# Output projection of the second attention block: both column halves per token tile, with one weight load asked for each pair of matmuls

## The chip, the cores and the metric

The kernel runs on one core of a Trainium2 chip. The metric is device time in microseconds (us), and lower is better. A "ratio" is the mean time of one kernel's fast runs over the mean time of the other kernel's fast runs in the same rounds, with a 95% interval, so it isn't quite the ratio of the medians that are quoted beside it.

The engines are named as in the profile: PE is the matmul engine (TensorE), PEld its weight loads, ACT is ScalarE, DVE is VectorE, POOL is GpSimd and SP is the engine that issues most DMAs (166 of the 176 issues in the trace before).

## The reference

Two independent attention blocks, A and B, have the same shapes. Their outputs are put side by side.

```python
# B=16 sequences, 32 query tokens, D=1024, 32 query heads, 4 key/value heads, 512 cached keys, head size 128; bf16
q = (x @ wq) split into heads
scores = q @ k_cache.T * 128 ** -0.5        # each key/value head serves 8 query heads
o = softmax(scores) @ v_cache
out = concat_heads(o) @ wo                  # [512 tokens, 4096] @ [4096, 1024]
result = concatenate([out_A, out_B], axis=-1)
```

The change touches the last product of block B alone. It is computed for four tiles of 128 tokens. Each tile needs 32 products (one per head) for each of two column halves of 512.

## The kernel before

PE interleaves two streams. In each "slot" it computes the scores of one (sequence, key/value head) and the weighted values of an earlier one. Between them it takes some 6.6 products from a generator, `stream()`, which delivers the query projections and then the output projections. So there is always a dense product ready while ACT and DVE work on the softmax.

```python
def f_units(pr, tt, n0, width, eng):                 # one token tile, one column half
    ps = psum.tile([P, NW], FP32, name="f_ps", tag="proj")      # "proj": 2 PSUM banks
    nh, off = divmod(n0, NW)
    for h in range(HQ):                              # 32 heads
        nc.tensor.matmul(
            ps[:, 0:width],
            lhsT=oT[pr, tt][:, h, :],                # stationary operand: attention output of a head
            rhs=wo_tiles[pr, nh, h // REP][:, h % REP, off:off + width],
            start=(h == 0), stop=(h == HQ - 1),
        )
        if h == HQ - 1:
            o_sb = outp.tile([P, NW], BF16, name="o_sb")
            nc.scalar.copy(out=o_sb[:, 0:width], in_=ps[:, 0:width])
            eng.dma_start(out=..., in_=o_sb[:, 0:width])
        yield

def run(units, n):
    for _ in range(n):
        next(units, None)
# ... (cut: query projections, scores, values, softmax sums)
for i in range(total_slots + LAG):
    if live:
        do_loads(i)        # DMA issues planned for this slot
        scores(i)          # 4 matmuls of 256 columns, then the exponential on ACT
    run(units, 1)
    # ...
    values(i - LAG)        # 4 matmuls of 256 columns
    # ...
    run(units, 5)
    # ...
```

Each stationary operand `oT[1, tt][:, h, :]` is thus loaded twice, once for either column half, at times that lie far apart. (For the last token tile it is three times: its second half is computed as two quarters of 256 columns.)

## Time and profile before

| | before |
|---|---|
| time, median of the first 3 runs | 343.30 us (342.92 to 343.53) |
| span of the profiled run | 341.2 us |
| PE busy | 335.2 us, 98% |
| weight loads (PEld) | 213.6 us, 63%, 2121 of them |
| ACT and DVE busy | 54% and 78% |

The first fence holds lines of the page of the kernel before: busy time with share and number of instructions of each engine, the granted TensorE clock in 40 equal slices (9 stands for 90% or more), the chain of work that ended last, and four groups of instructions. A group's line gives the line of the program, engine, operation, operands, count, then busy us and mean ns of one, then the idle time of the engine just before.

```profile
PE 335.2 (98%) x2082; PEld 213.6 (63%) x2121; DVE 265.5 (78%) x336; ACT 185.9 (54%) x209; POOL 46.7 (14%) x206
...
PEclk9999999999999999999999999999999999999999
...
PE 98%; issue 1%; ACT 0%; ACTq 0%
...
L320 PE MATMUL f_ps<-wo_sb,oT 128*128 128x512 bf16 (+1 forms) x525 | 128.2, 366 | 0.6
...
L425 PE MATMUL ob<-p_sb,v_sb 128*128 128x256 bf16 x512 | 76.8, 273 | 0.8
...
L320 PEld LDWEIGHTS <-oT 128*128 128x128 bf16 x544 | 53.2, 98 | 35.3
...
L425 PEld LDWEIGHTS <-v_sb 128*128 128x128 bf16 x512 | 50.1, 98 | 20.0
```

PE is never idle for long, its clock is full in every slice (the trace's record of it begins at 5.1 us), and the chain that ended last is PE nearly from end to end. A matmul's recorded time (366 ns on average here, 379 for one of 512 columns) is longer than the distance to the next start, so the records of successive matmuls overlap. The pace is read from starts. This is the timeline of PE alone (start, duration, then the group and its count), from the same trace:

```profile
200.32 1.46 PE L320 MATMUL f_ps<-wo_sb,oT 128*128 128x512 bf16 x6
201.61 0.60 PE L357 MATMUL s_ps<-qT,kT 128*128 128x256 bf16 x4
202.05 0.38 PE L320 MATMUL f_ps<-wo_sb,oT 128*128 128x512 bf16 x1
202.26 0.60 PE L425 MATMUL ob<-p_sb,v_sb 128*128 128x256 bf16 x4
```

Six products of 512 columns start at 200.32 and the next group at 201.61: 1.29 us / 6 = 215 ns each. Four of 256 columns take 201.61 to 202.05, 110 ns each. Taken from all records, the distance is 215 or 216 ns after 512 columns (mean 215.8) and 109 or 110 ns after 256 (mean 109.2). The 256 columns between them thus cost 106.7 ns, which is 2.4 columns per ns, and some 2.5 ns of either distance is left that doesn't grow with the columns. This rate and this remainder are what the recorded texts below write as "2.4 GHz" and "2.5 ns". Everywhere from the query projections of the stream to the last matmul there is nothing else, apart from some distances that are exactly a sum of two, where a record is missing (2082 matmuls were recorded, and 2121 loads).

### The profile page before, as it was taken

Reading aid. Unit: us, or ns where it says so; the run is one execution under the profiler, and the core shown is the slowest. Engines: PE = TensorE matmul, PEld = TensorE weight load, DVE = VectorE, ACT = ScalarE, POOL = GpSimd, SP = SyncE. Lnnn points to the kernel's source line nnn. Section 1 sums busy time; section 2 is a strip of 40 time slices with the busy share of each in tenths; the row PEclk is TensorE's granted clock in tenths of the full one; section 3 lists DMA queues with packets and bytes.
Section 4 is the critical chain, followed back from the end, with each engine's and each line's share of the span. In section 5 each row is a group of like instructions: output and inputs, shape, how many; then the busy total and the mean of one; then the engine's idle time right before and its main releaser. Section 6 shows DMA issues by size and latency. Waiting matters only on the chain.

```text
span 341.2 us, 5454 instructions
## 1 busy us (share of the span) xinstructions
PE 335.2 (98%) x2082; PEld 213.6 (63%) x2121; DVE 265.5 (78%) x336; ACT 185.9 (54%) x209; POOL 46.7 (14%) x206
## 2 busy tenths in 40 slices
PE   8999999999999999999999999999999999999996
PEld 6455666666666666666666666666666666666555
DVE  1046988888988898888888988879888888889540
ACT  3058666666667667666645545555555555555110
POOL 0001110011111111110012221222122101111100
PEclk9999999999999999999999999999999999999999
DMA  7999999999996987899999955998449997430001
GB/s 211 287 190 273 285 249 202 233 242 268 291 248 154 232 242 219 210 314 299 308 306 258 250 125 144 334 268 242 118 103 296 356 187 176 104 97 16 18 18 33
DMA packets 128094, 71.70 MB, mean 210 GB/s; under 512 B 75840, under 2 KB 127296, under 8 KB 128064
## 3 DMA queue, kind: packets, MB, share of 16 engines
q1 hardware_dynamic: 127264, 70.07, 84.1%
q0 software_dynamic: 384, 1.05, 0.9%
q8 instruction: 17, 0.28, 0.3%
q10 hardware_dynamic: 416, 0.20, 0.2%
q14 instruction: 13, 0.11, 0.1%
HBM read 50.86 MB, written 2.10 MB: 155 GB/s over the span
## 4 chain that ended last, share of the span: by engine, by line
PE 98%; issue 1%; ACT 0%; ACTq 0%
PE f_ps L320 32%; PE q_ps L301 28%; PE ob L425 17%; PE s_ps L357 16%; PE q_ps L534 4%; PE q_ps L516 1%; PE xT_ps L524 0%; ACT o_sb L329 0%; ACTq L329 0%
## 5 line engine op out<-in xcount | busy, mean ns | idle before, releaser
L365 ACT ACTIVATE p_sb<-s_ps,shift 128x1024 bf16<-128x1024 f32 x128 | 142.7, 1115 | 97.5 <-PE s_ps L357 88.1
L376 DVE TRANSPOSE_TENSOR_REDUCE parts<-p_sb 128x32 f32<-128x1024 bf16 x128 | 158.7, 1240 | 21.0 <-ACT p_sb L365 19.3
L320 PE MATMUL f_ps<-wo_sb,oT 128*128 128x512 bf16 (+1 forms) x525 | 128.2, 366 | 0.6
L301 PE MATMUL q_ps<-xT,wq_sb 128*128 128x512 bf16 x430 | 113.2, 379 | 0.5
L425 PE MATMUL ob<-p_sb,v_sb 128*128 128x256 bf16 x512 | 76.8, 273 | 0.8
L357 PE MATMUL s_ps<-qT,kT 128*128 128x256 bf16 x512 | 76.8, 273 | 0.0
L320 PEld LDWEIGHTS <-oT 128*128 128x128 bf16 x544 | 53.2, 98 | 35.3
L357 PEld LDWEIGHTS <-kT 128*128 128x128 bf16 x512 | 56.9, 113 | 28.3
L301 PEld LDWEIGHTS <-wq_sb 128*128 128x128 bf16 x448 | 43.8, 98 | 32.2
L425 PEld LDWEIGHTS <-v_sb 128*128 128x128 bf16 x512 | 50.1, 98 | 20.0
L447 DVE TENSOR_TENSOR oT<-r,ob 128x512 bf16<-128x512 f32 x64 | 43.9, 686 | 19.9 <-PE ob L425 19.4
L411 DVE STREAM_TRANSPOSE r<-rall 128x512 f32<-128x512 f32 x64 | 44.2, 691 | 1.1
L309 ACT CAST qT<-q_ps 128x512 bf16<-128x512 f32 x56 | 32.7, 583 | 16.5 <-PE q_ps L301 16.5
L394 POOL COPY half<-cs 64x32 f32<-64x32 f32 x32 | 6.5, 204 | 231.8 <-DVE cs L384 231.8
L329 ACT CAST o_sb<-f_ps 128x512 bf16<-128x512 f32 (+1 forms) x17 | 9.5, 559 | 23.6 <-PE f_ps L320 23.6
L534 PE MATMUL q_ps<-xT,w_sb 128*128 128x512 bf16 (+1 forms) x65 | 14.4, 379 | 0.1
L384 DVE TENSOR_REDUCE cs<-parts 128x32 f32<-128x128 f32 x32 | 12.1, 377 | 1.1
L406 DVE RECIPROCAL rall<-sums 128x32 f32<-128x32 f32 x32 | 10.2, 319 | 3.3 <-POOL sums L403 3.3
L534 PEld LDWEIGHTS <-w_sb 128*128 128x128 bf16 x67 | 6.8, 102 | 7.0 <-DMA w_sb<-in_A_wq_dram 0.2
L560 DVE CAST qT<-q_ps 128x512 bf16<-128x512 f32 x4 | 2.5, 684 | 10.2 <-PE q_ps L534 10.2
L331 POOL DMA_DIRECT2D out_dram<-o_sb x8 | 4.6, 574 | 29.3 <-ACT o_sb L329 29.3
L395 POOL TENSOR_TENSOR half<-half,cs 64x32 f32<-64x32 f32 x32 | 7.8, 243 | 2.6
(25 smaller groups left out, 44.7 us busy)
## 6 DMA issues: line engine op xcount, KB each, us to landing
v_sb<-in_A_v_cache_dram SPq DMA_DIRECT2D x16, 512.0 KB, 5.7
wq_sb<-in_B_wq_dram SPq DMA_DIRECT2D x8, 1024.0 KB, 5.7
wo_sb<-in_A_wo_dram SPq DMA_DIRECT2D x8, 1024.0 KB, 7.4
v_sb<-in_B_v_cache_dram SPq DMA_DIRECT2D x16, 512.0 KB, 4.7
wo_sb<-in_B_wo_dram SPq DMA_DIRECT2D x8, 1024.0 KB, 8.1
wq_sb<-in_A_wq_dram SPq DMA_DIRECT2D x5, 1024.0 KB, 5.8
wq_sb<-in_A_wq_dram SPq DMA_DIRECT2D x2, 512.0 KB, 6.7
kT<-in_A_k_cache_dram SPq DMA_TRANSPOSE x64, 4.4
```

The lines of the kernel that those rows point to most:

```text
L301: nc.tensor.matmul(ps[:], lhsT=w[:, dc, (h % 4) * DH:(h % 4 + 1) * DH], rhs=xT[pr][:, dc, :], start=(dc == 0), stop=(dc == DC - 1),)
L309: nc.scalar.copy(out=qT[pr, g][:, :, hl, :], in_=ps[:].rearrange("p (b s) -> p b s", s=SQ),)
L320: nc.tensor.matmul(ps[:, 0:width], lhsT=oT[pr, tt][:, h, :], rhs=wo_tiles[pr, nh, h // REP][:, h % REP, off:off + width], start=(h == 0), ...
L357: nc.tensor.matmul(s_ps[:, c, :], lhsT=kT[:, i % GRP, c, :], rhs=qT[pr, g][:, b, :, :].rearrange("p h s -> p (h s)"), start=True, stop=True,)
L365: nc.scalar.activation(out=p_sb[:], in_=s_ps[:], func=ACTF.Exp, bias=shift[:], scale=SCALE)
L376: nc.vector.tensor_reduce(out=parts[k][:, q, :, :].rearrange("p c h -> p (c h)"), in_=st[i]["p"][:].rearrange("p c (h s) -> p (c h) s", s=SQ),
L384: nc.vector.tensor_reduce(out=cs[:], in_=parts.pop(k)[:].rearrange("p q c h -> p q h c"), axis=AX.X, op=ALU.add,)
L406: nc.vector.reciprocal(out=rall[:, k, :], in_=quad.pop(k)[:])
L411: nc.vector.transpose(out=r[:].rearrange("p n s -> p (n s)"), in_=rall[:, k, o * 2 * REP:(o + 1) * 2 * REP] .unsqueeze(2).to_broadcast([P, ...
L425: nc.tensor.matmul(ob[j][:, q, :], lhsT=v_sb[:, i % GRP, c, :], rhs=st[i]["p"][:, c, :], start=(c == 0), stop=(c == KC - 1),)
L447: nc.vector.tensor_tensor(out=out, in0=rcp.pop(j)[:].rearrange("p (q h) s -> p q h s", h=REP), in1=ob.pop(j)[:].rearrange("p q (h s) -> p ...
L534: nc.tensor.matmul(first_q[h][:, ts], lhsT=w0[dc // HC][:, dc % HC, h * DH:(h + 1) * DH], rhs=xT[0][:, dc, ts], start=(dc == 0 and t0 == 0 ...
```

## The change

The intent is to compute both halves of a token tile together: for each head, one product for either half with the same stationary operand, where the second matmul is flagged to do without a weight load. The first half runs six heads ahead (`skew`), so that the two PSUM banks are not both due for eviction at once. The last token tile is paired without skew: its first half goes with the first quarter of its second half, and the last quarter stays alone. The second half of B's `wo` is needed right away, so it is loaded six slots earlier. The diff, cut to its core:

```diff
+            def f_pair(pr, tt, parts, skew, tag):
+                # ... (cut: two PSUM tiles, "proj", or one double tile "s" for the last token tile)
+                def product(k, h, first, last, reload=True):
+                    # ...
+                    mm = same_weights if not reload else nc.tensor.matmul
+                    mm(ps[k][:, 0:width], lhsT=oT[pr, tt][:, h, :], rhs=..., start=first, stop=last)
+                # ... (cut: leave(k): copy on ACT, DMA out on SP)
+                for h in range(skew):
+                    product(0, h, h == 0, False)
+                    yield 1
+                for h in range(skew, HQ):
+                    product(0, h, h == 0, h == HQ - 1)
+                    product(1, h, h == skew, skew == 0 and h == HQ - 1, reload=False)
+                    if h == HQ - 1:
+                        leave(0)
+                    yield 2
+                for h in range(skew):
+                    product(1, h, False, h == skew - 1)
+                    yield 1
+                leave(1)
+
+            def same_weights(out, lhsT, rhs, start, stop):
+                pe = nc.tensor
+                pe.add_instruction(mybir.InstMatmult(..., ldweights=False,
+                    ins=[pe.lower_ap(rhs), pe.lower_ap(lhsT)], outs=[pe.lower_ap(out)]))
+
+            credit = [0]
             def run(units, n):
-                for _ in range(n):
-                    next(units, None)
+                credit[0] += n
+                while credit[0] > 0:
+                    credit[0] -= next(units, None) or 1
@@ stream()
-                for tts in ((0, 1), (2,)):
-                    for nh in range(NH):
-                        for tt in tts:
-                            yield from f_units(1, tt, nh * NW, NW, nc.sync)
-                yield from f_units(1, TT - 1, 0, NW, nc.sync)
-                yield from f_units(1, TT - 1, NW, QW, nc.sync)
+                for tt in range(TT - 1):
+                    yield from f_pair(1, tt, ((0, NW), (NW, NW)), 6, "proj")
+                yield from f_pair(1, TT - 1, ((0, NW), (NW, QW)), 0, "s")
                 yield from f_units(1, TT - 1, NW + QW, QW, nc.scalar)
@@ planned loads
-                    at(NG + 20 + nh * 18 + hg, load_wo, 1, nh, hg)
+                    at(NG + 20 + nh * 12 + hg, load_wo, 1, nh, hg)
```

## The prediction

> **What bounds the kernel now.** TensorE, without a bubble. The page gives PE 98% busy (335.2 of 341.2 us), PEclk 9 in every slice, and a last-ended chain that is 98% PE. In the timeline of PE a 128x512 matmul is followed by the next start after 216 ns, a 128x256 one after 109 ns, from 7.5 us to the end; the few doubled distances (432, 325) are missing records (2082 matmuls against 2121 loads). 1024 wide x 216 + 1024 narrow x 109 ns = 332.8 us (an estimate from those distances and the counts in the code); start-up and the last eviction with its DMA are the rest. 512/2.4 GHz = 213.3 ns, so about 2.5 ns per matmul is not streaming. [...]
>
> **Is the weight load on the path?** No. The page shows PEld 213.6 us (63%), 98 ns each for oT, but it overlaps PE. [...] a 256-wide matmul with its own 98 ns load (the attention values, and the narrow last output products) still starts every 109 ns. At 216 ns the load has twice the room. Removing it frees nothing.
>
> **What the change removes.** Three pairs with 26 shared loads (32 less skew 6) and the last with 32: 110 loads, 110 x 98 ns = 10.8 us of PEld, none critical. If[...] the 2.5 ns belonged to the weight switch, 0.28 us.
>
> **What it adds and moves.** Matmul count and widths stay. A pair holds both "proj" PSUM buffers; the next pair's first write comes six products (1.3 us, plus 0.44 to 0.9 us of attention matmuls) after the eviction was released. That eviction is 0.58 us and may queue behind a 1.11 us exponential: about 1.7 us against 1.7 to 2.2 us. Three handovers: bubbles of 0 to 0.5 us in all. Wo's second half is loaded six slots (14 us) earlier, still seven slots before use, against 8.1 us to landing; by my count of live tiles the 20 buffers just suffice. Output DMAs come as neighbours on SP; the loads behind them lead by six slots. Last tile: two evictions at about 334.7 us instead of 331.2 and 334.7; their DMAs (1.8 us) land before the last product (338.2) and its own eviction and DMA, so the end is unchanged.
>
> **Prediction.** 343.2 us, range 342.4 to 344.4. Chances: faster by over 2% 0.01; within 2% 0.94; slower by over 2% 0.05.
>
> **What would show it.** Right: about 110 fewer PEld instructions and PEld busy near 203 us, while distances in the f products stay 216 ns and the span within 1 us. Wrong: distances of 213 ns after reused weights (the constant was the weight switch); idle time before f_ps matmuls, released by ACT o_sb (handover) or by a DMA of wo_sb (buffers).
>
> **What would make it wrong.** If a matmul without its own load kept the next load from being pulled ahead, each pair would expose up to 98 ns: 110 x 98 = 10.8 us, 3% slower. If an earlier Wo load waited for a buffer, SP would hold up the key and value loads behind it and PE would starve for several us.

## The result, and the profile after

| | before | after |
|---|---|---|
| median of 6 runs each | 343.41 us | 343.53 us |
| lowest to highest | 342.92 to 343.83 | 343.20 to 343.72 |
| ratio after/before, 95% interval | | 1.0003 (0.9991 to 1.0016) |
| span of the profiled run | 341.2 us | 341.9 us |
| "the stream": first query projection in it (L301) to last matmul, start to start | 318.957 us | 318.957 us |

The time is the same. The last row is stricter than the runs' spread: from the first query projection of the stream to the last output product, PE takes the same time to the nanosecond in both traces. The 0.7 us between the two profiled spans lies before that, where the first product of the stream starts at 18.91 us in one and 19.59 us in the other. The start-up code is the same in both. In the trace after, the last warm-up matmul is followed by the first transpose 453 ns later, in the trace before after 142 ns. There the profile charges 0.6 us of waiting of weight loads to the DMA that brings `x`, and then 0.5 us (before: 0.2) to the one that brings the first weights.

The page after, in the lines that answer to those before (the line numbers moved; L349 is `nc.tensor.matmul` in `product`, L383 the flagged matmul in `same_weights`, L320 the remaining `f_units`):

```profile
PE 335.6 (98%) x2081; PEld 213.7 (63%) x2121; DVE 265.5 (78%) x336; ACT 185.9 (54%) x209; POOL 46.7 (14%) x206
...
PEclk9999999999999999999999999999999999999999
...
PE 95%; DVE 1%; issue 1%; DMA 1%; ACT 0%; POOL 0%; ACTq 0%
...
L320 PEld LDWEIGHTS <-oT 128*128 128x128 bf16 x288 | 28.2, 98 | 17.7
L349 PEld LDWEIGHTS <-oT 128*128 128x128 bf16 x146 | 14.3, 98 | 11.7
L383 PE MATMUL f_ps<-wo_sb,oT 128*128 128x512 bf16 (+1 forms) x110 | 38.3, 348 | 0.4
L383 PEld LDWEIGHTS <-oT 128*128 128x128 bf16 x110 | 10.8, 98 | 6.3
```

The chain has 95% of PE here and 98% before. That is no new wait: followed back, it leaves PE at 232.5 us, where one matmul record is missing (a distance of 325 ns, exactly 216 + 109) and 53 ns look idle, and then runs through DVE and ACT for 9 us in which no start on PE is late. The 1% of DMA is the wait for `x`.

Here is the surprise. There are 2121 loads, as before, and 213.7 us of them. The 110 matmuls of L383, flagged to reuse the stationary operand, have 110 loads of their own under the same line. 288 + 146 + 110 = 544 loads of `oT`, just as many as before. The timeline of the changed kernel shows the same thing one by one, each L383 product behind its own load:

```profile
320.21 0.10 PEld L349 LDWEIGHTS <-oT 128*128 128x128 bf16 x1
...
320.43 0.38 PE L349 MATMUL f_ps<-wo_sb,oT 128*128 128x512 bf16 x1
320.43 0.10 PEld L383 LDWEIGHTS <-oT 128*128 128x128 bf16 x1
320.64 0.38 PE L383 MATMUL f_ps<-wo_sb,oT 128*128 128x512 bf16 x1
```

The compiled program says where they come from. This is its list of instructions for PE in a pair (not a profile):

```
L349 Ldweights oT
L349 Matmult f_ps<-wo_sb,oT 128x512
L383 Ldweights oT
L383 Matmult f_ps<-wo_sb,oT 128x512
```

In the compiled program each matmul is a load and a product, and the flagged ones have a load in front of them too: 2121 loads in this trace, for 2121 matmuls (the number in e1, where no record is missing). A build of the changed kernel with `nc.tensor.matmul` in place of `same_weights` gives a program of the same 14,998 instructions. Compared one by one, and names and line notes aside, none differs. So what ran is a reordering of the same work, and the outcome "same" doesn't yet say whether a load that is really left out would help.

### The profile page after: what moved, and what is told of

Its sections match the earlier page's. It is cut to its first block, busy times and chain, and to the rows that moved or that the text cites. A ratio compares the mean times of both kernels' runs of the same rounds, so it can differ in the third digit from the quotient of the medians.

```text
span 341.9 us, 5450 instructions
## 1 busy us (share of the span) xinstructions
PE 335.6 (98%) x2081; PEld 213.7 (63%) x2121; DVE 265.5 (78%) x336; ACT 185.9 (54%) x209; POOL 46.7 (14%) x206
## 4 chain that ended last, share of the span: by engine, by line
PE 95%; DVE 1%; issue 1%; DMA 1%; ACT 0%; POOL 0%; ACTq 0%
PE q_ps L301 28%; PE ob L481 17%; PE s_ps L413 16%; PE f_ps L320 15%; PE f_ps L349 9%; PE f_ps L383 6%; PE q_ps L590 4%; DMA x_sb<-in_A_x_dram 1%; DVE parts L432 1%; PE xT_ps L580 0%; ACT p_sb L421 0%; DVE r L467 0%; DVE oT L503 0%; DVE cs L440 0%; ACT o_sb L329 0%
## 5 line engine op out<-in xcount | busy, mean ns | idle before, releaser
L301 PE MATMUL q_ps<-xT,wq_sb 128*128 128x512 bf16 x430 | 113.2, 379 | 0.5
L320 PE MATMUL f_ps<-wo_sb,oT 128*128 128x512 bf16 (+1 forms) x277 | 69.3, 367 | 0.3
L301 PEld LDWEIGHTS <-wq_sb 128*128 128x128 bf16 x448 | 43.8, 98 | 32.2
L349 PE MATMUL f_ps<-wo_sb,oT 128*128 128x512 bf16 x137 | 46.4, 379 | 0.0
L320 PEld LDWEIGHTS <-oT 128*128 128x128 bf16 x288 | 28.2, 98 | 17.7
L383 PE MATMUL f_ps<-wo_sb,oT 128*128 128x512 bf16 (+1 forms) x110 | 38.3, 348 | 0.4
L450 POOL COPY half<-cs 64x32 f32<-64x32 f32 x32 | 6.5, 204 | 232.5 <-DVE cs L440 232.5
L349 PEld LDWEIGHTS <-oT 128*128 128x128 bf16 x146 | 14.3, 98 | 11.7
L383 PEld LDWEIGHTS <-oT 128*128 128x128 bf16 x110 | 10.8, 98 | 6.3
L360 ACT CAST o_sb<-f_ps 128x512 bf16<-128x512 f32 (+1 forms) x8 | 4.4, 557 | 17.7 <-PE f_ps L383 10.3
```

The lines of the kernel that those rows point to most:

```text
L301: nc.tensor.matmul(ps[:], lhsT=w[:, dc, (h % 4) * DH:(h % 4 + 1) * DH], rhs=xT[pr][:, dc, :], start=(dc == 0), stop=(dc == DC - 1),)
L320: nc.tensor.matmul(ps[:, 0:width], lhsT=oT[pr, tt][:, h, :], rhs=wo_tiles[pr, nh, h // REP][:, h % REP, off:off + width], start=(h == 0), ...
L349: mm(ps[k][:, 0:width], lhsT=oT[pr, tt][:, h, :], rhs=wo_tiles[pr, nh, h // REP][:, h % REP, off:off + width], start=first, stop=last,)
L383: pe.add_instruction(mybir.InstMatmult(name=nc.get_next_instruction_name(), engine=pe.engine, start_tensor_calc=start, stop_tensor_calc=st ...
```

## The experiments

Two questions were put to the chip. The first: is the load hidden, or was it merely never removed? My theory (theory 1) is that a load in front of a matmul runs under the matmul before it and costs the chain nothing. The rivals were that the 2.5 ns a matmul takes above 512 columns at 2.4 per ns is the change of weights (A), that a load costs its recorded 98 ns (B), and that a matmul without a load holds up the next load (C). The second question: did the moved parts (skew, earlier `wo`) do what the prediction said of them?

### e1: the loads really removed

The kernel's launch code takes the repeated loads out of the compiled program before it is handed on. The result is correct. A load with a wait attached stays, and so 108 of the 110 go.

```diff
+def _without_reloads(bir):          # drops an Ldweights of oT that repeats the one before it
+    # ... for each PE instruction:
+    #     if it is an Ldweights with the operand of the last one and no semaphore: leave it out
-    nc = _bacc.Bacc("TRN2", ...)
+    class Bacc(_bacc.Bacc):
+        def to_json_bytes(self):
+            return _without_reloads(super().to_json_bytes())
+    nc = Bacc("TRN2", ...)
```

> The changed kernel with 108 of its 110 second loads really taken out of the compiled program (the profile after still shows 2121 loads). Theory 1, the load is hidden under the running matmul: PEld x2013 instead of 2121 and about 10.6 us less PEld busy time, but distances of 216 ns after a reused operand too, stream from the first L301 product to the last product 318.96 us as in both kernels, ratio to before 1.000 (0.998 to 1.002). Rival A, the 2.5 ns above 512/2.4 GHz is the weight switch: distances of 213.3 ns before a matmul that reuses, stream shorter by 108 x 2.5 = 0.27 us. Rival B, a load costs its 98 ns and was merely never removed: stream shorter by up to 10.6 us, ratio 0.97. Rival C, a matmul without its own load blocks the pull-ahead of the next load: stream longer by up to 10.6 us, ratio 1.03.

Measured: 343.24 us against 343.50, ratio 0.9993 (0.9979 to 1.0006). The page of e1:

```profile
PE 337.0 (99%) x2121; PEld 202.7 (59%) x2013; DVE 265.6 (78%) x336; ACT 185.9 (54%) x209; POOL 46.7 (14%) x206
```

The loads fell to 2013 and by 11 us. PE's busy time is no witness here: it is 1.4 us higher, in a trace in which no matmul record is missing (2121 of 2121). The timeline of e1 shows flagged products (L383) with no load of their own; the load of the next head starts together with them:

```profile
319.41 0.38 PE L383 MATMUL f_ps<-wo_sb,oT 128*128 128x512 bf16 x1
319.41 0.10 PEld L349 LDWEIGHTS <-oT 128*128 128x128 bf16 x1 [0.23 <-issue]
...
319.62 0.38 PE L349 MATMUL f_ps<-wo_sb,oT 128*128 128x512 bf16 x1
319.84 0.38 PE L383 MATMUL f_ps<-wo_sb,oT 128*128 128x512 bf16 x1
319.84 0.10 PEld L349 LDWEIGHTS <-oT 128*128 128x128 bf16 x1 [0.33 <-issue]
```

The starts are 0.21 to 0.22 us apart whether a load stands between or not: of 78 distances from a product to its flagged partner, 71 are 216 ns and 7 are 215. The stream takes 318.957 us, again the same to the nanosecond. Theory 1 holds and all three rivals fall. In particular the 2.5 ns is not the change of weights: the distance is 215 or 216 ns where the weights don't change, too.

### e2: every load doubled

An idle load of the same operand goes in front of each of the 544 output products.

```diff
+                    nc.tensor.ldweights(oT[pr, tt][:, h, :])   # in f_units and in product
                     nc.tensor.matmul(...)
```

> The changed kernel with a second, idle load of the same operand before each of the 544 output products (512 wide and 64 narrow or fewer). Theory 1: a 216 ns matmul has room for two loads, so PEld x2665, PE distances stay 216 ns, ratio 1.000. Rival B (a load costs its time on the chain): 544 x 98 ns = 53 us longer, ratio 1.16. If a load keeps its reader for its whole 98 ns, the wide products still have room (196 < 216), but the 64 narrow ones of the last tile (109 ns) go to 196 ns, 5.6 us longer, ratio 1.016.

Measured: 343.63 us against 343.50, ratio 0.9999 (0.9983 to 1.0014). The page of e2:

```profile
PE 338.0 (99%) x2121; PEld 230.1 (67%) x2665; DVE 265.6 (78%) x336; ACT 185.7 (54%) x209; POOL 46.7 (14%) x206
```

544 more loads change nothing. The distances stay 215 or 216 ns, those of the 256-column products 109 or 110 with two loads each, and the stream takes 318.957 us. The timeline of PE in e2 shows the last 32 of these as one group:

```profile
335.27 3.66 PE L321 MATMUL f_ps<-wo_sb,oT 128*128 128x256 bf16 x32
```

Less the last one's recorded 0.27 us, this is 3.39 us for 31 distances, 109 ns each. The variant in which a load keeps its reader for the whole 98 ns would have shown 196 ns there.

### e3 and e4: pieces of 64 columns, with a load each and without

How narrow must a product be before its load shows? B's paired products are cut into 1920 pieces of 64 columns with the same stationary operand. In e3 each piece has its load. In e4 the repeated ones are removed as in e1.

```diff
-                    mm(ps[k][:, 0:width], lhsT=oT[pr, tt][:, h, :], rhs=..., start=first, stop=last)
+                    for p0 in range(0, width, 64):
+                        # matmul of columns p0 to p0+64, started only with the first piece's first head
```

> Every paired product of B cut into 64-column pieces of the same stationary operand, each piece with a load of its own: 1920 pieces in place of 256 products. Theory 1 says that a load is hidden as long as it is shorter than the matmul before it. 64/2.4 GHz + 2.5 ns = 29 ns (an estimate from the 216 and 109 ns distances) is surely shorter than a load, so here the loads must bind: distances of 53 ns if a load takes one column per 2.4 GHz cycle (1920 x 53 = 102 us in place of 52, ratio 1.15), 98 ns if it is exclusive for the whole recorded time (188 us, ratio 1.40); the 56 ns distances of the start-up transposes say at most 56. If even here distances are 29 ns, loads are never visible.

> The same pieces with all second and later loads of the same operand taken out of the compiled program (1771 of them). Theory 1: distances of 29 ns within a product, so about 1920 x 29 = 56 us in place of 52, ratio to before 1.01, and far faster than the pieces with loads. If an instruction floor binds instead, the distance shows it (say 50 ns: ratio 1.13).

Measured: e3 349.94 us, ratio 1.0199 (1.0167 to 1.0230); e4 347.92 us, ratio 1.0123 (1.0107 to 1.0138); before 343.50. My number for e3 was wrong by far: I had said that here the loads must bind, at 53 ns or more, and that e4 would be far faster. The timelines of PE and then PEld in e3:

```profile
296.48 1.56 PE L350 MATMUL f_ps<-wo_sb,oT 128*128 128x64 bf16 x48
...
296.38 1.55 PEld L350 LDWEIGHTS <-oT 128*128 128x128 bf16 x48
```

and of PE and PEld in e4:

```profile
297.34 0.63 PE L350 MATMUL f_ps<-wo_sb,oT 128*128 128x64 bf16 x16
...
297.23 0.10 PEld L350 LDWEIGHTS <-oT 128*128 128x128 bf16 x1
```

With a load each, 48 pieces take 1.56 us, of which the last one's recorded 193 ns is overhang: (1.56 - 0.19) / 47 = 29 ns. Without, 16 take (0.63 - 0.19) / 15 = 29 ns. Over all records 29 or 30 ns is the distance in both. So a load whose own record is 98 ns long is hidden where the matmuls start 29 ns apart: the records of successive loads overlap each other (48 of 98 ns in 1.55 us) as those of matmuls do.

What then makes e3 2 us slower than e4? Its stream is 325.40 us long and e4's 323.66. Both pay 1664 more matmuls x 2.5 ns = 4.2 us (an estimate from the counts and the distances). In e4 0.4 us more is one wait for a `wq` DMA in the query projections. In e3 there is a single distance of 1.95 us between two score matmuls (and one of 0.33 us between two pieces), which the profile charges to "issue", that is, to nothing that it shows:

```profile
L415 PE MATMUL s_ps<-qT,kT 128*128 128x256 bf16 x512 | 77.1, 273 | 1.7 <-issue 1.7
```

The queue q8, which the profile lists as "instruction", moved 30 packets in e3, 23 in e4 and 17 in the kernel before. A packet of q8 has 16,384 bytes, and there are some 250 recorded PE instructions (loads and matmuls) to a packet (7570 / 30 in e3, 4203 / 17 before). The two long distances of e3 lie exactly 2048 = 8 x 256 such instructions apart, and those of e9 below 256, 257 and 256; each ends 1.3 to 1.5 us after the end of a q8 packet. I suspect that PE ran out of fetched instructions there. The traces show where the long distances lie; the cause they do not show, and no run changes the fetching alone.

### e5 and e8: more than one load per gap

As e3, but only the last token tile's pair is cut (384 pieces, after the loop, where nothing else runs on PE for most of the time), with four loads of the same operand before each piece in e5 and two in e8.

```diff
+                    if tt == TT - 1:
+                        for p0 in range(0, width, 64):
+                            for _ in range(3):                  # e8: range(1)
+                                pe.ldweights(oT[pr, tt][:, h, :])
+                            # the piece, which brings its own load
```

> The pieces of 64 columns with one load each kept 29 ns, so the pace of the loads is still unknown, only that it is 29 ns or less. Here only the last token tile's pair (after the loop, nothing interleaved) is cut into 384 pieces of 64 columns, each behind four loads of the same operand. If a load holds up the chain only by its own pace L, the distance of the pieces is the larger of 29 ns and 4 x L: 98 ns each (exclusive) 392 ns, which the last runs already exclude; 29 ns 116 ns[...]. The tail of 384 pieces is then about 384 x (distance - 27 ns) longer than the 10.4 us of the changed kernel: [...]34 us for 116 ns. Distances of 29 ns would mean that repeated loads of one operand are not made at all.

> As the run with four loads per piece, but two. There the pieces stood 137 ns apart before the clock was halved: 29 ns as with one load, and 108 ns for three more, 36 ns each. Theory: one load is hidden under the matmul before it, and every further one of the same gap is paid for with 36 ns; so 29 + 36 = 65 ns. Rival: all loads share one pace of 137/4 = 34 ns, so 2 x 34 = 68 ns (and one load per piece should have shown 34, which it did not); or a fixed surcharge, which would give about 137 again.

Measured, one run each (and so of unknown state): e5 399.24 us, e8 358.43 us, beside 343.02 and 342.96 for the kernel before. So loads are not free when several come in a row before a short piece. In e5 the first twenty or so pieces stand 137 ns apart at full clock: 29 ns as with one load, and (137 - 29) / 3 = 36 ns for each further one. In e8 the distances are nearly all 57 to 65 ns with a mean of 60 (and one of 480 ns, charged to "issue", which doesn't fit the count of 256), so the second load costs about 31 ns. The expectation of 65 was somewhat high, and the rivals' 68 and 137 don't fit either. But this is the price at 64 columns, not the price of a load: in e2 every 256-column output product had two loads as well and stayed at 109 or 110 ns. What fits all runs is that the loads between two matmuls are hidden as long as together they need less time than the matmul, at some 30 to 34 ns a load when they come in a row (60 / 2, 137 / 4), while a single one fits into 25 ns (e9). That is read out of these runs and not tested by one of its own. One load per matmul was hidden at every width tried: 512, 256, 64 and 32 columns, 216, 109, 29 and 25 ns apart.

e5 showed one more thing. The table of stretches of e5 (us, then busy time and count of PE, PEld, DVE, ACT and POOL, granted clock, DMA share, GB/s):

```profile
320.00:324.70 4.70, 4.70 (x29) 2.76 (x30) 2.46 (x4) 0.58 (x1) 0.65 (x3) 1.00 0.04 11
324.70:327.90 3.20, 3.20 (x25) 3.20 (x94) 0.00 (x0) 0.59 (x1) 0.00 (x0) 1.00 0.21 73
328.70:340.00 11.30, 11.30 (x70) 11.30 (x272) 3.76 (x9) 0.00 (x0) 0.00 (x0) 0.50 0.01 3
```

The first piece starts at 324.80 us. After 3.3 us of such pieces the granted clock falls to 0.50 (at 328.07 us), the distances are 166 to 167 ns, and it stays so to the last piece at 388.6 us and 4.3 us beyond, though PE counts as busy throughout. Of the 55 us by which e5's stream is longer than that of the kernel before, some 42 us are the price of the pieces at 137 ns (384 x (137 - 27), an estimate); the rest came with the clock, which the expectation had not foreseen. Columns stream in only 27 of each 137 ns (64 columns at the 2.4 per ns of the distances, an estimate). In e8, where they stream in 27 of 60, the clock stays 1.00:

```profile
330.00:334.00 4.00, 4.00 (x73) 4.00 (x142) 0.31 (x2) 0.00 (x0) 0.00 (x0) 1.00 0.01 4
```

PE is 100% busy in the stretches of both runs, so the busy share doesn't tell the two apart. What made the clock fall was not shown: e5 is one run, and no cause was tested.

### e9 and e10: pieces of 32 columns

The last pair cut into 768 pieces of 32 columns, with a load each (e9) and with the repeated ones removed (e10).

```diff
-                        for p0 in range(0, width, 64):
+                        for p0 in range(0, width, 32):          # e10: and loads removed as in e1
```

> The last token tile's pair cut into 768 pieces of 32 columns, one load each. 32/2.4 GHz + 2.5 ns = 16 ns (an estimate from the 216, 109 and 29 ns distances)[...]. Theory: a load of 36 ns no longer fits under such a piece, so distances are 29 to 40 ns here, and fewer without the loads. If they are 25 ns or less, a single load is hidden even here.

> The same 768 pieces with the repeated loads taken out of the compiled program: distances of 16 ns (no floor) or 25 ns[...]. The difference to the run with loads is what reuse is worth at this width; theory 4 to 24 ns a piece, rival none.

Measured, one run each (of unknown state): e9 355.67 us, e10 352.40 us, beside 342.96 for the kernel before. The timeline of PEld and PE in e9:

```profile
325.91 8.18 PEld L352 LDWEIGHTS <-oT 128*128 128x128 bf16 x321
326.02 8.15 PE L352 MATMUL f_ps<-wo_sb,oT 128*128 128x32 bf16 x320
```

and of PE in e10:

```profile
325.83 8.33 PE L352 MATMUL f_ps<-wo_sb,oT 128*128 128x32 bf16 x327
```

(8.15 - 0.18) / 319 = 25 ns with loads, (8.33 - 0.18) / 326 = 25 ns without. So 25 ns is the distance with and without loads, above the 16 ns of the estimate in e9's expectation; what sets it was not shown. The 25 ns in the two expectations rested on no run of this case. My 29 to 40 ns for e9 was wrong: a single load is hidden even at this width. The price of e9's loads is elsewhere: its 768 pieces have four long distances of 0.36 to 0.85 us, 2.4 us in all, charged to "issue"; e10 has none. These are the four that lie 256 or 257 PE instructions apart; as in e3, the cause is not shown. For each piece e9 issues two PE instructions where e10 mostly issues one.

### e6: without the skew

```diff
-                    yield from f_pair(1, tt, ((0, NW), (NW, NW)), 6, "proj")
+                    yield from f_pair(1, tt, ((0, NW), (NW, NW)), 0, "proj")
```

> The changed kernel with skew 0: both halves start and end together. Theory: at each of three handovers the first products of a pair must wait for evictions that were released one product (216 ns) before, 0.58 us of ACT and up to one 1.11 us exponential ahead of them: 0.5 to 2.4 us of PE idle time before f_ps products at each, released by ACT o_sb, 2 to 5 us in all, ratio 1.006 to 1.015. If the skew is not needed (rival: attention work fills the wait), PE shows no idle time and the ratio is 1.000.

Measured: 346.78 us against 343.02, ratio 1.0101 (1.0084 to 1.0118). The stream is 3.48 us longer. One handover in the timeline of e6:

```profile
282.39 1.07 ACT L360 CAST o_sb<-f_ps 128x512 bf16<-128x512 f32 x2
...
283.02 0.38 PE L349 MATMUL f_ps<-wo_sb,oT 128*128 128x512 bf16 x1 [0.81 <-ACT o_sb L360]
...
283.50 0.38 PE L383 MATMUL f_ps<-wo_sb,oT 128*128 128x512 bf16 x1
```

PE waits 0.81 us for the first bank and then a little for the second; over the three handovers, the excess of the distances is 0.62 us, 0.97 + 0.27 us and 0.19 + 1.44 us, which is the whole 3.5 us. So the pairing by itself costs 1%, and the skew of six products is what buys that back. In the changed kernel no distance at a handover is longer than it should be, so six were enough.

### e7: the second half of `wo` at its old place

```diff
-                    at(NG + 20 + nh * 12 + hg, load_wo, 1, nh, hg)
+                    at(NG + 20 + nh * 18 + hg, load_wo, 1, nh, hg)
```

> The changed kernel with the second half of Wo loaded in the slots of the kernel before (102 to 105 in place of 96 to 99). There the four landed at 265.1, 268.4, 271.4 and 274.4 us, and the changed kernel wants the first at 261.7 us and the second about 1 us later. Theory: PE waits for DMAs of wo_sb, 5 to 7 us in all, ratio 1.015 to 1.020. So the earlier load is a price that the pairing needs, not a gain. Rival: the SP queue issues early enough anyway, ratio 1.000.

Measured: 350.24 us against 343.02, ratio 1.0213 (1.0189 to 1.0236), a little more than expected. In the profiled run, the fastest of the four at 348.73 us, the stream is 5.10 us longer. The group that waited, and then stretches of e7 in the columns used for e5:

```profile
L383 PE MATMUL f_ps<-wo_sb,oT 128*128 128x512 bf16 x78 | 30.0, 384 | 3.5 <-DMA wo_sb<-in_B_wo_dram 3.1
```

```profile
261.00:265.00 4.00, 0.89 (x6) 0.28 (x4) 1.86 (x3) 0.65 (x1) 1.24 (x6) 1.00 1.00 325
265.00:268.00 3.00, 3.00 (x12) 1.60 (x13) 0.35 (x1) 1.11 (x1) 0.04 (x1) 0.57 1.08 371
```

PE stands still for about 3.3 us until the first piece of `wo` is there. Half a microsecond after it has started again the granted clock falls to 0.50, from 265.43 to 268.85 us (0.57 is the mean of the stretch shown). Distances in that time are 213 ns after 256 columns, and at the second piece 739 ns, of which 427 is what 512 columns take at that clock (twice 213), so some 0.3 us is waiting. That makes 3.6 us of waiting; the other 1.5 us of the 5.10 us are the halved clock: a cost that I had not put into the expectation, which was near in size but counted all of it as waiting. The other three runs have a mean clock of 0.990 against 0.995 in this one. This trace shows one fall of the clock, after a stop of 3.3 us; that the stop caused it was not tested. In the changed kernel the four loads landed at 246.1, 249.1, 256.5 and 259.5 us, ahead of their first use at 261.7 us.

## Why the prediction was right, point by point, and where it was not

- **What bounds the kernel: right.** PE without a bubble, at a distance fixed by the columns (216 ns at 512, 109 at 256). Four kernels (before, after, e1, e2) have the same stream to the nanosecond.
- **"Removing it frees nothing": right, but the result alone did not show it.** The change removed no load, so the time would have come out the same however dear a load was; on this point the agreement of the number was luck. It took e1. With 108 loads out, the ratio is 0.9993 and the distance stays 216 ns; with 544 more in, it is 0.9999.
- **"110 fewer PEld instructions and PEld busy near 203 us": wrong.** After the change there are 2121 loads and 213.7 us. The prediction took the flag in the source for the program. The compile step puts the load back. In e1, where they are gone, the figures are what was written: 2013 loads and 202.7 us.
- **The alternative of 0.28 us for the weight switch: refuted** by distances of 216 ns after a reused operand (e1).
- **The risk of 10.8 us if a matmul without its own load keeps the next load back: refuted** by e1, where the next load still starts with the flagged product (319.41 us, 0.10 us long) and ends well before its matmul (319.62 us).
- **The argument that a load's 98 ns fit under the matmul above it: right here, but the 98 ns are the wrong measure.** Loads recorded at 98 and 96 ns are hidden under matmuls 29 and even 25 ns apart (e3, e9). At 64 columns, further loads of the same gap cost some 31 to 36 ns each (e5, e8); a second one under 256 or 512 columns cost nothing (e2).
- **The handovers and the earlier load: right.** "Bubbles of 0 to 0.5 us in all" was 0, and e6 and e7 show what each precaution holds off: 3.5 us, and 5 us and more.
- **The end unchanged: right.** From the last matmul's end to the end of the span it is 3.08 us in both traces.

A large gain was never there to be had. 1024 matmuls x 213.3 ns + 1024 x 106.7 ns of streaming columns are 327.7 us (an estimate from the counts and the 2.4 columns per ns of the distances), 95% of 343.5 us.

## What to carry to other kernels

Before saving weight loads, look at the distance between matmul starts with the load in place. Here it grew with the columns and left 2.5 ns over, the load was hidden, and a shorter list of loads bought nothing: PEld's share was 59%, 63% and 67% in e1, before and e2, with the time the same (ratios 0.9993 in e1 and 0.9999 in e2). When a change asks for an operation to be left out, count it in the profile after: an unchanged time may come from a change that never reached the chip. Pairing two accumulations needed its own precautions (staggered evictions, operands loaded earlier), which here cost nothing when present (ratio 1.0003) and 1 to 2% when missing (1.0101 in e6, 1.0213 in e7).
